# Recurrent attention with streamed weights: 14 buffers hold two weight pieces by turns, head halves swap order, softmax by rows, and a separate stage for the batched tokens' output projection

## The chip, the cores and the metric

One core of a Trainium2 chip runs one program. The metric is the device time of one execution in microseconds. The engines are TensorE (PE), VectorE (DVE), ScalarE (ACT), GpSimd (POOL) and SyncE (SP); DMAs are issued from the queues of SP, ACT and POOL.

## The reference, cut to what matters

```
x: [2048, 1024]; Wq, Wk, Wv: [1024, 32 heads, 128]; Wo: [32, 128, 1024]
mem = mem0                                   # 8 rows
for s in range(64):                          # 32 tokens per segment
    h = concat(mem, x[32*s : 32*s + 32])     # 40 rows
    q, k, v = h @ Wq, h @ Wk, h @ Wv         # per head
    scores = where(idx_q < 8 or idx_q >= idx_k, q k^T * 128**-0.5, -1e9)
    o = softmax(scores) @ v, then @ Wo       # 40 x 1024
    mem = o[:8];  outs.append(o[8:])
a = concat(outs)
b = (gelu(x @ w_gate) * (x @ w_up)) @ w_down # 3584 hidden columns
g = sigmoid(sum(x * gate_w))
out = g * a + (1 - g) * b
```

All inputs and the output are bf16. The 64 segments depend on each other through `mem`, so they run one after the other. The four weight matrices of the attention are 8 MB each, 32 MB together, and more than the on-chip buffers hold.

## The kernel before, in words

**Three stages.** A prologue loads and transposes x, computes the gate, and computes q, k and v of the "rest" tokens: of each segment's 32 tokens the last 8 (`NB`) are projected in one batch for all segments, 512 rows, and written to scratch tensors in HBM (`qk_scr`, `v_scr`). Then comes the loop over 64 steps (one segment each), whose projections carry 32 rows: 24 tokens of the segment and the 8 memory rows. Last comes the feed-forward stage (matmuls at L941 and L978), which also mixes in the attention result.

**Pieces.** Each weight matrix is cut into 16 pieces of 512 KB ([128, 2048] bf16): half `u` of the heads (16 heads) times 8 slices of the contraction (for Wo: 8 pairs of heads per half). A step walks all 64 pieces in the order of `pos` (L301): k half 0, q half 0, k half 1, q half 1, v half 0, v half 1, then Wo half 0 and half 1. A q, k or v piece is four matmuls of 32 output rows by 512 columns (L793), one for each quarter of the PE's columns, which run side by side. A Wo piece is eight matmuls of 256 columns (L819), two rounds of four.

**Residents and ring.** 44 pieces stay in SBUF for the whole loop (`res`). The other 20 (`streamed`, L308) are loaded again in each step into a ring of 5 buffers (`ring`). `load_str` (L342) issues the next ring load on SP's queue when the piece that held the buffer has been used; SP's instructions run in the order in which they were written, so a load waits for its buffer and all later loads wait behind it.

**Softmax.** The batched tokens' columns of k and q are put beside the step's own (`put_rest`, POOL, from `qkr`). For each half `u`, `scores` (L686) computes masked scores with queries on partitions only for the row maximum (DVE, L700). `scores_T` computes them again with keys on partitions. `shift` and `denom` subtract the maximum and sum over keys by matmuls with a block matrix of ones, with two exponentials and a logarithm on ACT (L741, L753, L759). `attend` (L762) multiplies by v, and four copies (ACT and DVE by turns) bring the result to `oT`.

**Order of the work.** Helpers are hung on piece numbers (`on(n, f)`, L841 on): they are written into the program ahead of piece n. Each engine runs its instructions in program order and waits on semaphores.

**Wo.** Each step multiplies all 32 rows by Wo into bank A0. The 8 batched tokens' rows are collected over four steps (`keep_o` into `oTR`), and in every fourth step `proj` does a second set of matmuls for them with the same pieces, into bank A1 (`lag`), which POOL stores (`a_scr<-a_rb`).

**End of a step.** The Wo result is copied to `a_bf` (half by ACT, half by DVE), transposed on the PE (L890) and copied by DVE into the memory columns of the next step's `hT` (L893); the next step's first matmul waits for that copy.

**Prologue details that the change touches.** The q and k results of the rest tokens are gathered in `stq` and stored to `qk_scr` by a DMA on ACT's queue, 2 MB in runs of 256 B. Some v pieces are loaded into `tmpv`, which lies over `stq`, by SP (L571). The v results go to `v_scr` by SP's DMAs from `stv` (L558).

Of the kernel before, what the change touches and what calls it, by code (L numbers as in the profile page):

```python
# [195 lines left out]
def bass_gated_mix__memory_aug_recurrent_mem_tr__geglu_ffn__prompt_kernel(  # L196
# [19 lines left out]
    SEG = 32  # L216
# [8 lines left out]
    NRING = 5  # L225
# [6 lines left out]
    with ExitStack() as es:  # L232
# [12 lines left out]
        v_scr = nc.dram_tensor("v_scr", [NSEG // 2, 4, 32, 512], BF16)  # L245
# [19 lines left out]
        bones = al("bones", [128, 128])  # L265
        delta = al("delta", [128, 32])
        mS = al("mS", [128, 80])
        mT = al("mT", [128, LQ])
        mR = al("mR", [128, 4, 16])
        gal = al("gal", [128, NT], FP32)  # L270
        hT = [al(f"hT{i}", [128, KC, 32]) for i in range(2)]
        a_bf = al("a_bf", [128, 256])
        nm = [al(f"nm{u}", [128, 4, 2], FP32) for u in range(2)]
        qkr = al("qkr", [128, 4, 128])
        oTR = [al(f"oTR{u}", [128, 4, 4, 32]) for u in range(2)]
        a_rb = al("a_rb", [128, 256], at=oTR[0].off)
        low = cur[0] = (cur[0] + 63) // 64 * 64
        vB = al("vB", [128, 4, 128])

        xb = [al(f"xb{i}", [128, 640]).off for i in range(4)]  # L280
        kT = [al(f"kT{u}", [128, 4, 4, LQ], at=xb[(0, 2)[u]]) for u in range(2)]
        qT = [al(f"qT{u}", [128, 4, 4, LQ], at=xb[1]) for u in range(2)]
        DDs = [al(f"DD{u}", [128, 4, LQ], at=xb[(0, 2)[u]]) for u in range(2)]
        EE = [al(f"EE{u}", [128, 4, 56], at=xb[(0, 2)[u]]) for u in range(2)]
        LN = [al(f"LN{u}", [128, 4, LQ], FP32, at=xb[(0, 2)[u]] + 448) for u in range(2)]
        oT = [al(f"oT{u}", [128, 4, 4, LQ], at=xb[(1, 0)[u]]) for u in range(2)]
        tok = al("tok", [128, 512], at=xb[3])
        vA = [al(f"vA{u}", [128, 4, 128], at=xb[3]) for u in range(2)]
# [12 lines left out]
        pos = [(m, u, kc) for m, u in QUADS for kc in range(KC)]  # L301
        pos += [("o", u, g, jj) for u in range(2) for g in range(4) for jj in range(2)]
        assert len(pos) == 64
        at_, tot = [], 0
        for p in range(64):
            tot += 1 + extra.get(p, 0)
            at_.append(tot)
        streamed = [(at_[p] * NSTR) // tot > ((at_[p - 1] if p else 0) * NSTR) // tot for p in range(64)]  # L308
        assert sum(streamed) == NSTR
        res = {p: al(f"res{p}", [128, 2048]) for p in range(64) if not streamed[p]}  # L310
        str_pos = [p for p in range(64) if streamed[p]]
        str_qkv = [p for p in str_pos if p < 48]
        seq = [p for p in str_qkv if p < 32] + str_pos * NSEG
# [16 lines left out]
        def dst(t, p):  # L330
            return t[:, :].rearrange("p (h f) -> p h f", h=2) if pos[p][0] == "o" else t[:, :]
# [692 lines left out]
```

## Time and profile before

| what | value |
|---|---|
| median of 3 runs | 2887.17 us (2876.43 to 2901.04) |
| span of the profiled execution, its own time | 2881.1 us |
| PE busy | 2355.2 us (82%) |
| DVE, ACT, POOL busy | 757.5 us (26%), 627.0 us (22%), 337.8 us (12%) |
| DMA bytes | 838.19 MB, mean 291 GB/s |
| chain that ended last, by engine | DMA 47%, PE 43%, issue 4%, DVE 2% |
| chain, longest lines | ring<-Wq 17%, ring<-Wv 13%, L941 11%, L793 11%, L819 8%, ring<-Wk 7%, ring<-Wo 6% |

The profiled execution has no time of its own beside its span; the median of the timed runs is 6.1 us above the span. "Busy" is the union of an engine's instructions, and pipelined matmuls overlap, so a busy PE is not a PE at its peak rate. In a chain row, "DMA x" means that the work at that point waited for that transfer to land. Releasers are inferred.

### The profile page before, as it was taken

The page shows a single profiled execution, that of the slowest core. Times are in us where ns is not written, and L with a number is a line of the kernel's source. Part 1 is how long each engine was busy: PE and PEld are TensorE (multiplying, and loading weights), DVE is VectorE, ACT ScalarE, POOL GpSimd, SP SyncE. Part 2 cuts the span into 40 slices and gives each one's busy share as a digit, 9 for nine tenths or more (in the row PEclk, how much of TensorE's full clock was granted, in tenths as well). Part 3 has the DMA queues.
Part 4 walks back from the last instruction along what each step waited for, and adds up shares of the span by engine and source line. Part 5 has one row for each costly group of instructions (what it writes and reads, how often), then busy time and mean ns, then how long its engine had stood idle before and what let it go on. Part 6 is the DMA issues. An engine that isn't in the chain of part 4 may idle for free.

```text
span 2881.1 us, 88022 instructions
## 1 busy us (share of the span) xinstructions
PE 2355.2 (82%) x40448; PEld 1097.0 (38%) x40486; DVE 757.5 (26%) x1829; ACT 627.0 (22%) x1461; POOL 337.8 (12%) x775
## 2 busy tenths in 40 slices
PE   7687788787787877787787877787777899999998
PEld 3333333343333333333343333333333444444443
DVE  1411222112222212222222221222212353526262
ACT  1211222222222222222222221222222231303130
POOL 2400111111111111111111111111111000000000
PEclk9888998999999999999999999999999999999999
DMA  9546999999999999999999999999999926070705
GB/s 336 168 155 237 368 356 341 321 333 348 341 362 345 377 345 342 363 349 361 335 343 351 335 351 333 361 345 342 347 331 357 367 78 225 1 245 4 245 4 190
DMA packets 338595, 838.19 MB, mean 291 GB/s; under 512 B 65193, under 2 KB 79529, under 8 KB 338225
## 3 DMA queue, kind: packets, MB, share of 16 engines
q1 hardware_dynamic: 284512, 789.16, 76.3%
q0 software_dynamic: 13824, 22.16, 2.4%
q10 hardware_dynamic: 39888, 21.24, 2.4%
q8 instruction: 317, 5.19, 0.7%
q14 instruction: 54, 0.43, 0.0%
HBM read 806.11 MB, written 26.21 MB: 289 GB/s over the span
## 4 chain that ended last, share of the span: by engine, by line
DMA 47%; PE 43%; issue 4%; DVE 2%; ACT 1%; POOL 1%; ACTq 1%; SPq 0%; POOLq 0%
DMA ring<-in_A_Wq_dram 17%; DMA ring<-in_A_Wv_dram 13%; PE pb L941 11%; PE pb L793 11%; PE pb L819 8%; DMA ring<-in_A_Wk_dram 7%; DMA ring<-in_A_Wo_dram 6%; PE pb L978 6%; PE pb L517 2%; DMA wd<-in_B_w_down_dram 1%; PE pb L545 1%; PE pb L674 1%; POOL gp L475 1%; DMA qk_scr<-stq 1%; ACTq L472 1%
## 5 line engine op out<-in xcount | busy, mean ns | idle before, releaser
L793 PE MATMUL pb<-res,hT 128*32 128x512 bf16 x8448 | 671.2, 404 | 2.0 <-issue 2.0
L793 PE MATMUL pb<-ring,hT 128*32 128x512 bf16 x3840 | 403.1, 409 | 286.1 <-DMA ring<-in_A_Wk_dram 103.7
L793 PEld LDWEIGHTS pb<-ring,hT 128*32 128x32 bf16 x3840 | 102.0, 95 | 487.6 <-DMA ring<-in_A_Wk_dram 165.5
L793 PEld LDWEIGHTS pb<-res,hT 128*32 128x32 bf16 x8448 | 215.6, 100 | 165.6 <-issue 43.2
L819 PE MATMUL pb<-res,oT 128*32 128x256 bf16 x5632 | 247.7, 281 | 37.7 <-issue 37.4
L657 ACT ACTIVATE tok<-pb 128x512 bf16<-128x512 f32 (+1 forms) x256 | 139.2, 544 | 583.0 <-PE pb L793 577.5
L941 PE MATMUL pb<-xT,wg 128*128 128x512 bf16 x896 | 211.8, 379 | 9.5 <-DVE GT L957 8.4
L941 PE MATMUL pb<-xT,wu 128*128 128x512 bf16 x896 | 211.7, 379 | 0.0
L978 PE MATMUL pb<-wd,GT 128*128 128x512 bf16 x876 | 194.2, 379 | 7.4 <-DMA wd<-in_B_w_down_dram 6.1
L819 PE MATMUL pb<-ring,oT 128*32 128x256 bf16 x2560 | 140.9, 283 | 54.0 <-DMA ring<-in_A_Wo_dram 24.6
L819 PEld LDWEIGHTS pb<-res,oT 128*32 128x32 bf16 x5632 | 150.8, 99 | 60.0 <-issue 49.0
L949 ACT ACTIVATE s<-pb 128x512 f32<-128x512 f32 x112 | 66.8, 596 | 316.2 <-PE pb L941 296.7
L831 POOL COPY oTR<-oT 128x128 bf16<-128x128 bf16 x128 | 37.6, 294 | 828.3 <-DVE oT L660 828.3
L700 DVE TENSOR_REDUCE nm<-pb 128x8 f32<-128x320 f32 x128 | 63.0, 492 | 270.4 <-PE pb L696 270.4
L941 PEld LDWEIGHTS pb<-xT,wg 128*128 128x128 bf16 x896 | 86.9, 98 | 117.5 <-DVE GT L957 12.8
L978 PEld LDWEIGHTS pb<-wd,GT 128*128 128x128 bf16 x896 | 86.7, 98 | 115.0 <-DMA wd<-in_B_w_down_dram 12.0
L941 PEld LDWEIGHTS pb<-xT,wu 128*128 128x128 bf16 x896 | 87.7, 98 | 105.7
L657 ACT ACTIVATE oT<-pb 128x160 bf16<-128x160 f32 x256 | 63.8, 301 | 273.6 <-PE pb L774 273.6
L660 DVE CAST oT<-pb 128x160 bf16<-128x160 f32 x256 | 71.2, 320 | 197.9 <-PE pb L774 197.9
L826 POOL COPY qT<-qkr 128x128 bf16<-128x128 bf16 x128 | 45.0, 351 | 587.6 <-PE pb L720 582.5
L950 DVE SCALAR_TENSOR_TENSOR tp<-s,pb 128x512 f32<-128x512 f32 x112 | 77.0, 687 | 137.2 <-ACT s L949 137.1
L819 PEld LDWEIGHTS pb<-ring,oT 128*32 128x32 bf16 x2560 | 61.4, 97 | 119.9 <-issue 56.3
(106 smaller groups left out, 2493.0 us busy)
## 6 DMA issues: line engine op xcount, KB each, us to landing
ring<-in_A_Wk_dram SPq DMA_DIRECT2D x325, 512.0 KB, 6.2
ring<-in_A_Wq_dram SPq DMA_DIRECT2D x325, 512.0 KB, 7.2
ring<-in_A_Wv_dram SPq DMA_DIRECT2D x320, 512.0 KB, 6.7
ring<-in_A_Wo_dram SPq DMA_DIRECT2D x320, 512.0 KB, 6.7
wd<-in_B_w_down_dram SPq DMA_DIRECT2D x56, 1024.0 KB, 6.0
qk_scr<-stq ACTq DMA_DIRECT2D x4, 2048.0 KB, 11.6
qkr<-qk_scr POOLq DMA_DIRECT2D x64, 128.0 KB, 6.1
res<-in_A_Wk_dram SPq DMA_DIRECT2D x11, 512.0 KB, 12.2
```

Source lines behind the costliest of these rows:

```text
L517: ins = e.matmul(PB[b][:, 0:NRT], lhsT=w8[kc][:, c:c + 128], rhs=xrT[:, kc, :], start=(kc == 0), stop=(kc == KC - 1))
L657: op("act", lambda e: e.activation(o, i, ACTF.Copy), rd=rd, wr=wr)
L660: op("dve", lambda e: e.tensor_copy(o, i), rd=rd, wr=wr)
L700: op("dve", lambda e: e.tensor_reduce(nm[u][:, :, :].rearrange("p a b -> p (a b)"), PB[SS][:, 0:320].rearrange("p (a c) -> p a c", c=LQ), ...
L793: ins = e.matmul(PB[bk][32 * g:32 * g + 32, :], lhsT=h[:, kc, :], rhs=w[:, g * 512:(g + 1) * 512], start=(kc == 0), stop=(kc == KC - 1))
L819: ins = e.matmul(PB[bk][32 * g:32 * g + 32, 0:256], lhsT=o[u][:, gp_, 2 * jj + hh, 0:32], rhs=w[:, c:c + 256], start=(p == 48 and hh == 0) ...
L826: op("pool", lambda e: e.tensor_copy(t[:, :, :, 32:40].rearrange("p j g c -> p (j g) c"), qkr[:, m, :].rearrange("p (x c) -> p x c", c=8)) ...
L831: op("pool", lambda e: e.tensor_copy(oTR[u][:, :, :, 8 * i:8 * i + 8].rearrange("p g j c -> p (g j) c"), oT[u][:, :, :, 32:40].rearrange(" ...
L941: ins = e.matmul(PB[bk][:, 0:FB], lhsT=w[:, kc, cc:cc + 128], rhs=xT[:, :, :, kc, :].rearrange("p t i c -> p (t i) c"), start=(kc == 0), s ...
L949: op("act", lambda e, hg=hg: e.activation(s1[:, :], hg, ACTF.Square, scale=SQ), rd=[BK(bg)], wr=[s1.r()])
L950: op("dve", lambda e, hg=hg, t=t: e.scalar_tensor_tensor(out=t[:, :], in0=s1[:, :], scalar=1.0, in1=hg, op0=ALU.add, op1=ALU.mult), rd=[BK ...
L978: ins = e.matmul(PB[bank[2 * k + hf]][:, :], lhsT=GT[:, j, tb * 128:(tb + 1) * 128], rhs=w[:, jj, hf * 512:(hf + 1) * 512], start=(j == 0) ...
```

## The change

The 5 ring buffers are gone. There are 50 buffers (`slots`); 36 hold one piece for good, and 14 (`PAIRS`: 3 of k, 3 of q, 4 of v, 4 of Wo) hold the pieces of both head halves with the same contraction slice by turns. A step takes half `s % 2` first and the other half second, so the half that a shared buffer holds at the end of a step is the one that the next step begins with. `spent` issues the reload of a shared buffer behind the use of its piece.

The order of a step becomes k, q, v of the first half, k and q of the second, Wo of the first, v of the second, Wo of the second (`ORDER`). Only one set of `kT`, `qT`, `oT`, `tok` remains, and many small tiles lie over each other (`pA`, `pB` over `kT`; `E8`, `tA`, `tB` over `qT`; `a_bf` over `oT`; `vA` over `tok`).

The softmax works on the scores with queries on partitions: maximum, subtraction in PSUM, one exponential, sum, reciprocal, two multiplications, and two 32x32-block transposes, all but the exponential on DVE. `scores_T`, `shift` and `denom` with their masks are gone.

The batched tokens' rows of `oT` are collected in `oRc` and stored to `o_scr` in each step; a new stage between the loop and the feed-forward stage loads them (`oR`), reloads four Wo pieces (`xo`) and does 256 matmuls of 512 columns. In the prologue the halves are taken in the other order, v_scr is stored in runs of 256 B, and reloads follow `spent`.

```diff
-        ring = [al(f"ring{i}", [128, 2048]) for i in range(NRING)]
...
+        ORDER = (("k", 0), ("q", 0), ("v", 0), ("k", 1), ("q", 1), ("o", 0), ("v", 1), ("o", 1))
+        walk = [(m, r, i) for m, r in ORDER for i in range(8)]
+        def at_step(p, s):
+            m, r, i = (pos if s < 0 else walk)[p]
+            return (m, r ^ (s % 2), i)
+        PAIRS = {"k": (1, 3, 5), "q": (0, 2, 5), "v": (0, 2, 4, 6), "o": (0, 2, 4, 6)}
...
+        def fetch(n):
+            k, t = uses[n][done[n]], slots[n]
+            if paired(k):
+                lane = f"sl{n}"
...
+            op("sp", lambda e: e.dma_start(dst(t, k), src(k)), wr=[t.r()], lane=lane)
+        def spent(k):
+            n = home[k]
+            done[n] += 1
+            if done[n] < len(uses[n]) and uses[n][done[n]] != k:
+                fetch(n)
...
+            op("pool", lambda e: e.memset(pB[:, :].bitcast(FP32), 0.0), wr=[pB.r()])
+            op("dve", lambda e: e.tensor_reduce(nm, sS, AX.X, ALU.max, negate=True), rd=[BK(SS)], wr=[st8.r(0, 8)])
+            op("dve", lambda e: e.tensor_tensor(out=sS, in0=sS, in1=b8(nm, LQ), op=ALU.add), rd=[BK(SS), st8.r(0, 8)], wr=[BK(SS)])
+            op("act", lambda e: e.activation(E8[:, :, :].rearrange("p a c -> p (a c)"), PB[SS][:, 0:320], ACTF.Exp, scale=scale),
+               rd=[BK(SS)], wr=[E8.r()])
+            op("dve", lambda e: e.tensor_reduce(sm, E8[:, :, :], AX.X, ALU.add), rd=[E8.r()], wr=[st8.r(8, 16)])
+            op("dve", lambda e: e.reciprocal(sm, sm), rd=[st8.r(8, 16)], wr=[st8.r(8, 16)])
+            op("dve", lambda e: e.tensor_tensor(out=pA[:, :, :], in0=E8[:, :, 0:32], in1=b8(sm, 32), op=ALU.mult),
+               rd=[E8.r(), st8.r(8, 16)], wr=[pA.r()])
+            fin = op("dve", lambda e: e.tensor_tensor(
...
+            op("dve", lambda e: e.transpose(tA[:, :, :].rearrange("p a c -> p (a c)"), pA[:, :, :].rearrange("p a c -> p (a c)")),
+               rd=[pA.r()], wr=[tA.r()])
+            op("dve", lambda e: e.transpose(tB[:, :, :].rearrange("p a c -> p (a c)"), pB[:, 0:256]),
+               rd=[pB.r()], wr=[tB.r()], after=[fin])
...
         def attend(u):
-            bo = (T1, SS, (ST0, ST1)[u], XX)
+            bo = (B0, B1, B2, SS)
...
+                for g in range(4):
+                    r = slice(32 * g, 32 * g + 32)
+                    ins = e.matmul(PB[bo[g]][:, 0:4 * LQ].rearrange("p (j c) -> p j c", j=4)[:, :, 24:40], lhsT=vB[r, u, :],
...
+            op("pool", lambda e: e.tensor_copy(oRc[:, :, 16 * u:16 * u + 16].rearrange("p c x -> p x c"),
+                                               oT[:, :, :, 32:40].rearrange("p g j c -> p (g j) c")),
+               rd=[oT.r()], wr=[oRc.r()])
...
             def start_step():
-                put_rest(kT[0], 1)
-                put_rest(qT[0], 0)
-                put_rest(kT[1], 3)
+                put_rest(kT, 1)
+                put_rest(qT, 0)
                 for f in pend:
                     f()
                 pend.clear()
...
+                load_qk(s, 1)
+            def rest_1():
+                put_rest(kT, 1)
+                put_rest(qT, 0)
+                if not last:
+                    load_qk(s + 1, 0)
+            on("k", 0, 2, start_step)
+            on("k", 0, 5, lambda: load_h(s + 1) if not last else None)
+            on("q", 0, 0, lambda: evac(bko["k", 0], tok, "act"))
+            on("q", 0, 4, lambda: trans(kT, "dve"))
+            on("v", 0, 0, lambda: evac(bko["q", 0], tok, "act"))
+            on("v", 0, 3, lambda: trans(qT, "dve"))
+            on("v", 0, 7, lambda: scores())
+            on("k", 1, 0, lambda: evac(bko["v", 0], vA, "act"))
+            on("q", 1, 4, lambda: attend(ua))
+            on("q", 1, 5, lambda: rest_1())
+            on("q", 1, 5, lambda: evac(bko["k", 1], tok, "act"))
+            on("q", 1, 7, lambda: trans(kT, "dve"))
+            on("o", 0, 0, lambda: evac(bko["q", 1], tok, "act"))
+            on("o", 0, 3, lambda: trans(qT, "dve"))
+            on("o", 0, 7, lambda: scores())
+            on("o", 1, 0, lambda: evac(bko["v", 1], vA, "act"))
+            on("o", 1, 0, lambda: attend(ub))
+            on("o", 1, 0, lambda: load_v(s + 1) if not last else None)
...
-            act_copy(a_bf[:, 0:128], PB[A0][:, 0:128], [BK(A0)], [a_bf.r(0, 128)])
-            dve_copy(a_bf[:, 128:256], PB[A0][:, 128:256], [BK(A0)], [a_bf.r(128, 256)])
+            act_copy(a_bf[:, :], PB[XO][:, 0:256], [BK(XO)], [a_bf.r()])
...
+                op("pool", lambda e: e.dma_start(o_scr[s], oRc[:, :, :].rearrange("p c x -> p (c x)")), rd=[oRc.r()],
+                   wr=[("D", "o", s)], lane="sto")
...
+        load_oR(NBK - 1)
+        for b in range(NBK):
+            rb = rbs[b % 2]
+            for hf in range(2):
...
+                    for n, (u, i, hh) in enumerate((u, i, hh) for u in range(2) for i in range(8) for hh in range(2)):
+                        w = xo.get(("o", u, i)) or slots[home["o", u, i]]
+                        x = 16 * u + 2 * i + hh
+                        ins = e.matmul(PB[bk][0:RB, :], lhsT=oR[b][:, :, x],
+                                       rhs=w[:, hh * 1024 + hf * 512:hh * 1024 + hf * 512 + 512], start=(n == 0), stop=(n == 31))
...
+        load_w(2)
         load_w(3)
         load_w(4)
```

In the last step `early` holds `load_xo`, three `load_oR`, `load_xT(0)`, `load_w(0)` and `load_w(1)`; `oR` and `xo` lie over the buffers of v.

## Rows read from the trace of the kernel before

**Rows 1.** The page, 40 equal slices: busy share of the DMA engines, in tenths.

```profile
DMA  9546999999999999999999999999999926070705
```

**Rows 2.** The page, DMA issues: count, KB each, median us from issue to landing.

```profile
ring<-in_A_Wk_dram SPq DMA_DIRECT2D x325, 512.0 KB, 6.2
ring<-in_A_Wq_dram SPq DMA_DIRECT2D x325, 512.0 KB, 7.2
ring<-in_A_Wv_dram SPq DMA_DIRECT2D x320, 512.0 KB, 6.7
ring<-in_A_Wo_dram SPq DMA_DIRECT2D x320, 512.0 KB, 6.7
...
qk_scr<-stq ACTq DMA_DIRECT2D x4, 2048.0 KB, 11.6
...
a_scr<-a_bf POOLq DMA_DIRECT2D x64, 64.0 KB, 5.8
```

**Rows 3.** Tile hT: the copy that opens each next step, first and last start.

```profile
L893 DVE COPY hT<-pb x63: 191/192/193, 291.4 to 2238.4; 128x64 bf16<-128x64 bf16 x63
```

**Rows 4.** Stretches: us, PE, PEld, DVE, ACT, POOL busy, PEclk, DMA share, GB/s.

```profile
1050.00:1350.00 300.00, 234.56 (x5622) 109.55 (x5614) 65.55 (x207) 68.76 (x180) 41.95 (x99) 0.99 0.98 358
20.00:40.00 20.00, 19.95 (x91) 8.76 (x92) 3.77 (x6) 3.15 (x6) 6.54 (x24) 1.00 1.04 400
1578.90:1610.30 31.40, 25.47 (x532) 11.41 (x532) 6.64 (x21) 6.38 (x17) 3.63 (x9) 0.82 0.94 332
```

**Rows 5.** Timeline 1400 to 1435 us: start, us, engine, line, operation.

```profile
1404.42 0.38 PE L696 MATMUL pb<-kT,qT 128*32 128x40 bf16 x32
...
1413.75 1.06 PE L819 MATMUL pb<-res,oT 128*32 128x256 bf16 x32
...
1415.26 0.28 ACT L657 ACTIVATE a_bf<-pb 128x128 bf16<-128x128 f32 x1 [2.27 <-PE pb L819]
...
1416.48 0.40 PE L793 MATMUL pb<-ring,hT 128*32 128x512 bf16 x4 [0.28 <-DVE hT L893]
...
1418.82 1.04 PE L793 MATMUL pb<-res,hT 128*32 128x512 bf16 x16
...
1419.79 0.40 PE L674 MATMUL pb<-ident,tok 128*128 128x128 bf16 x4
...
1425.06 1.50 PE L793 MATMUL pb<-res,hT 128*32 128x512 bf16 x12
```

**Rows 6.** DMA issues, 186 to 200 us, the queue empty at first: us to landing.

```profile
tmpv<-in_A_Wv_dram SPq DMA_DIRECT2D x1, 512.0 KB, 4.3
```

**Rows 7.** Groups by shape, 1350 to 1650 us: busy, mean ns | idle before.

```profile
L700 DVE TENSOR_REDUCE nm<-pb 128x8 f32<-128x320 f32 x18 | 8.9, 492 | 35.5 <-PE pb L696 35.5
L756 DVE SCALAR_TENSOR_TENSOR pb<-pb,LN 128x160 f32<-128x160 f32 x18 | 6.0, 333 | 6.2 <-ACT LN L753 6.1
L657 ACT ACTIVATE tok<-pb 128x512 bf16<-128x512 f32 x30 | 17.9, 597 | 84.1 <-PE pb L793 84.1
```

**Rows 8.** PE's waits in the prologue, 0 to 262 us.

```profile
PE pb L517 <- DMA ring<-in_A_Wq_dram: 26.2, 1, 26.2
PE pb L545 <- ACT stv L552: 10.5, 1, 10.5
```

**Rows 9.** Timeline of SP's queue, 110 to 262 us.

```profile
134.32 0.33 SPq L571 DMA_DIRECT2D tmpv<-in_A_Wv_dram  x1
...
136.82 1.49 SPq L349 DMA_DIRECT2D ring<-in_A_Wq_dram  x2
...
189.84 0.33 SPq L571 DMA_DIRECT2D tmpv<-in_A_Wv_dram  x1
```

**Rows 10.** Timeline of PE, 244 to 270 us: the loop's first matmuls.

```profile
245.48 0.40 PE L793 MATMUL pb<-ring,hT 128*32 128x512 bf16 x4
```

**Rows 11.** The chain that ended last: feed-forward begins, and 49 matmuls of it.

```profile
2274.29 25.86 PE pb L941 x119
...
2822.43 10.74 PE pb L978 x49
```

More of the change, by code (lines that the diff above doesn't have):

```diff
@@ L284, in bass_gated_mix__memory_aug_recurrent_mem_tr__geglu_ffn__prompt_kernel @@
[L284 to L288, printed above, removed]
+        low = cur[0] = (cur[0] + 63) // 64 * 64
+        qkr = al("qkr", [128, 2, 128])
+        oRc = al("oRc", [128, NB, 32])
@@ new lines, in bass_gated_mix__memory_aug_recurrent_mem_tr__geglu_ffn__prompt_kernel @@
+        PAIRS = {"k": (1, 3, 5), "q": (0, 2, 5), "v": (0, 2, 4, 6), "o": (0, 2, 4, 6)}
+        hosts = []
+        for m in "kqvo":
+            for i in range(8):
+                if i in PAIRS[m]:
+                    hosts.append([(m, 0, i), (m, 1, i)])
+                else:
+                    hosts += [[(m, 0, i)], [(m, 1, i)]]
+        assert len(hosts) <= NSLOT, (len(hosts), NSLOT)
+        slots = [al(f"sl{n}", [128, 2048]) for n in range(len(hosts))]
+        home = {p: n for n, h in enumerate(hosts) for p in h}
@@ L315, in bass_gated_mix__memory_aug_recurrent_mem_tr__geglu_ffn__prompt_kernel @@
+        paired = lambda p: len(hosts[home[p]]) > 1
+        uses = [[] for _ in hosts]
+        for s_ in [-1] + list(range(NSEG)):
+            for p in range(48 if s_ < 0 else 64):
+                k = at_step(p, s_)
+                if s_ < 0 and k[0] == "v" and paired(k) and k[1] == 1:
+                    continue
+                uses[home[k]].append(k)
         P = _Prog(nc, new_sem, "a")
@@ L500, in bass_gated_mix__memory_aug_recurrent_mem_tr__geglu_ffn__prompt_kernel @@
         for n, (mat, u) in enumerate(QUADS):
-            w8 = [tmpv.get(8 * n + kc) or piece(8 * n + kc) for kc in range(KC)]
+            u = 1 - u
+            k8 = [(mat, u, kc) for kc in range(KC)]
+            w8 = [tmpv.get(k) or slots[home[k]] for k in k8]
             if mat != "v":
@@ L860, in bass_gated_mix__memory_aug_recurrent_mem_tr__geglu_ffn__prompt_kernel @@
-            on(26, lambda: scores(0))
-            on(28, lambda: scores_T(0, s % 2))
-            on(29, lambda: trans(tok, T0, kT[1], "act"))
-            on(32, lambda: evac(A1, tok, "both"))
-            on(32, lambda: shift(0))
-            on(35, lambda: trans(tok, T1, qT[1], "both"))
-            on(36, lambda: denom(0))
-            on(40, lambda: scores(1))
-            on(40, lambda: cp["act"](vA[0][:, :, :].rearrange("p j c -> p (j c)"), PB[A0][:, :], [BK(A0)], [vA[0].r()]))
-            on(41, lambda: scores_T(1, s % 2))
@@ L870, in bass_gated_mix__memory_aug_recurrent_mem_tr__geglu_ffn__prompt_kernel @@
-            on(44, lambda: attend(0))
-            on(44, lambda: keep_o(0, s % 4))
-            on(46, lambda: shift(1))
-            on(48, lambda: cp["dve"](vA[1][:, :, :].rearrange("p j c -> p (j c)"), PB[A1][:, :], [BK(A1)], [vA[1].r()]))
-            on(49, lambda: denom(1))
-            on(55, lambda: attend(1))
-            on(55, lambda: keep_o(1, s % 4))
-            on(56, lambda: load_v(s + 1) if s % 2 and not last else None)
+                load_qk(s, 1)
[4 more added lines that the diff above has]
+                    load_qk(s + 1, 0)
```

384 lines of the change are left out of this document (146 added, 238 removed).

## The prediction

> **What bounds the kernel now.** I read the page first. Its chain of waits is 47% DMA, nearly all of it ring loads, though PE is busy 82% of the span; so the busy share misleads, and the 40 slices say why: through the loop the DMA engines stand at 9 tenths in every slice [rows 1]. The list of DMA issues shows what they carry: 1,290 ring loads of 512 KB [rows 2], 20 in each of 64 steps and 10 in the prologue. The copy that opens a step runs from 291.4 to 2238.4 us [rows 3], 62 steps of 31.40 us. Twenty loads at the loop's 358 GB/s (DMA share 0.98) [rows 4] are 20 x 1.46 = 29.3 us, and about 1 us of small transfers makes 30.3: the loop is bound by reload bytes. PE's own work is far less: four pieces take 1.04 us with their drain and one takes 0.40 [rows 5], so a piece costs 0.213 us and 64 pieces 13.6 us.
>
> **Part 1, the reloads.** By the code a shared buffer changes its piece once in a step, between the first and the second half, so 14 reloads replace 20. They are no longer spread evenly: ten (k, q, v) are released in the first 24 pieces and queue up, and the four of Wo queue behind them. SP's next reload always belongs to a later release, so a blocked SP delays nothing. PE never outruns the last Wo reload by my count below, so a step is one round through it:
> - after that reload lands, two Wo pieces and their drain: 2 x 0.213 + 0.19 = 0.62 us;
> - the step's end to the next first matmul: now 1.22 us (1415.26 to 1416.48) [rows 5]. ACT copies twice the columns (0.28 grows to about 0.38) and the 0.30 of DVE behind it goes: 1.0 us;
> - k pieces 0 and 1, whose second releases the first reload: 0.62 us;
> - issue 0.1 us, and landing from an idle queue 4.3 us [rows 6]; the nearest other row is a ring load's 6.2 us behind others [rows 2], the upper end;
> - 13 more reloads. In the loop the rate is 358 GB/s, with up to five loads in flight; in the prologue, with more queued, 400 [rows 4]. That bounds one between 1.31 and 1.46 us. Ten will be queued here, but small transfers run beside them: I take the middle, 1.38, so 17.9 us;
> - six small transfers of 64 KB (hT, k and q of two halves, v, two stores), 1.0 us; they could fall into the pause of the reloads and cost nothing.
>
> Sum 25.5 us; with the low ends 23.7, with the high ends 28.5 (small transfers 1.0 and 1.2 us more for a slower clock at the round's PE parts). 63 steps: 1606 us.
> The Trainium skill ("DMA: Bandwidth & Descriptors", section "Where 436 GB/s comes from") says that loads from HBM are bound near 358 GB/s per core. The trace has 400 in one stretch [rows 4]; by the page's figure the step would be 26.6 us and the total some 70 us higher.
>
> **Part 2, the softmax.** PE loses `scores_T`, `shift`, `denom` and the second Wo set; all of it lay beside loads and gives nothing by itself. What is added is serial: from the end of `scores` DVE reduces (0.49 us [rows 7]), adds over 320 columns in PSUM (between 0.33, its 160-column neighbour, and 0.49; I take 0.49), ACT's exponential of 320 columns (under 0.60; 0.44), reduce 0.49, reciprocal 0.15, multiplications 0.33 and 0.2, two transposes that no row shows (0.2 to 0.5 each; 0.35), hand-overs 0.3: C = 3.6 us, from 2.6 to 7.2 if everything new is twice as dear. Cover of the first half: 12 pieces, 2.6 us; of the second: 9 pieces, 1.95 us. PE's serial path without any DMA wait is then 13.6 + transposes 4 x 0.2 + scores 2 x 0.5 [rows 5] + attends 0.8 + end 1.0 + stalls behind the copies of tok (0.60 each [rows 7]) and oT 1.9 + (C - 2.6) + (C - 1.95) = 14.6 + 2C = 21.8 us. That is below 25.5, so reloads cover it; without them it would be the step. Queued behind new waits: on ACT the copy of v behind the exponential (q's first piece needs its bank); on POOL `put_rest` behind the `oRc` copy (the k copy of DVE waits for it, under 1 us). A store of `a_bf` now holds `oT`, but lands in 5.8 us [rows 2], and `attend` comes some 11 us into the step. POOL also gets one memset per half, one more store and more loads; it idles most of the step.
>
> **Part 3, the prologue.** PE now waits 26.2 us for a ring load of Wq [rows 8], which SP issues at 136.82 only behind `tmpv` (134.32), which waits for a store of `stq` [rows 9]. The new order issues those q pieces a quad earlier: gone. The 10.5 us wait behind the first store of `stv` [rows 8] is SP stuck at the same line; v pieces will still queue ahead of that store, so I take half. Gain 31 us, between 10 and 37. v_scr in runs of 256 B costs nothing: `stq`, in such runs, takes 11.6 us for 2 MB [rows 2], so 0.7 us per 128 KB store, beside 55 us of matmuls (8 blocks of 32 at 0.219); without that cover, 23 us. The loop then begins at 245.5 [rows 10] - 31 = 214.5. In step 0 the twelve Wo pieces that had no room before load ahead of its 14 reloads: 26 x 1.38 + 4.4 + 1.0 + 2.2 = 43.5 us; it ends at 258, against 291.4.
>
> **Part 4, the new Wo stage.** In the last step the four `xo` pieces and the first `oR` can start only when v's buffers are free, behind the Wo reloads: 4 x 1.38 + 4 (1 MB in 512 B runs, 2.6 to 5.8 us by 400 GB/s and by the `stq` row) = 9.5 us, less 1.0 that the loop's tail covers: 8.5. Then 256 matmuls at 10.74 / 49 = 0.219 us [rows 11]: 56.1 us, on the path. The last `oR` load waits for the last store, with w2 to w4 and wd behind it on SP; the stage covers those, and w3 is wanted some 48 us into the feed-forward stage. Now the same multiplications hide under loads, and only 1.7 us lie between loop and feed-forward. Together 65 us.
>
> **Sum.** 258 + 63 x 25.5 + 65 + feed-forward as before (2881.1 - 2274.3 = 606.8) [rows 11] = 2536 us against the profiled 2881.1. The timed median is 6.1 us above that span, so 2542.
>
> **Rivals.**
> 1. *The serial softmax sets the step.* From C = 5.4 us PE's path passes 25.5. At C = 7.2 the step is 29.0 and the time 2542 + 63 x 3.5 = 2760. For it: both halves share one set of buffers, so nothing else fills PE. Against: each new operation has a near neighbour below 0.5 us [rows 7].
> 2. *Reloads cheaper than thought.* If the landing overlaps and the rate is above 400 GB/s, PE's 21.8 us is the step: 2542 - 63 x 3.7 = 2310. Against: the last Wo reload is tied to a release late in the step.
> 3. *Slower: PE's clock stays low.* The waits now bunch, in q of the second half and in the last Wo pieces. At 1.2 GHz twelve matmuls of three pieces take 1.50 us [rows 5], about 0.43 a piece. If that held, the path would be 27.3 of pieces + 7 of the rest, 34.5 us a step, and the time 2542 + 63 x 9 = 3110. It decides against the change where a step passes (2881 - 607 - 65 - 258) / 63 = 31.0 us, a mean granted clock near 0.6. Against: before, with waits for loads too, stretches have 0.99, and one of the lowest steps 0.82 [rows 4]. The Trainium skill ("TensorE: Matmul & The Clock Gate", section "What's actually happening") calls the half rate the default that activity lifts; the trace agrees that the clock falls after waits, and shows it coming back.
>
> That the reloads don't fall to 14 I exclude: the count follows from the code.
>
> **Chances.** Forecast 0.82 (its own range 2430 to 2720: the step's ends, -1.8 and +3.0 us times 63, with the prologue's and the new stage's partly offsetting), rival 1 beyond that 0.09, rival 2 0.05, rival 3 0.04. Runs of this kernel spread by about 1%, so 1% is what can be told from no change. Faster by over 1% is all but rival 3 and a little of rival 1: 0.94; the same 0.02, slower 0.04.
>
> **What would show it.** Right: 14 shared-buffer loads a step, hT copies 25.5 us apart, PE waiting in the last Wo pieces for shared buffers of Wo, a pause of the DMA engines around each step's start, and 56 us of 512-column Wo matmuls. Wrong: PE waiting for the transposed probabilities ahead of `attend` while its next reload has landed (rival 1); the last Wo pieces without a wait (rival 2); granted clock under 0.7 in the loop (rival 3); PE still idle for 20 us near 130 us (part 3).

## The result, and the profile after

The kernel before took 2881.8 us in the median of four runs, the changed one 2735.4 (2718.4 to 2737.6): a ratio of 0.948, 95% interval 0.943 to 0.953. The forecast was 2542, with a range that ended at 2720. The change made the kernel faster, as forecast; what failed is the length of a step.

The profiled execution has a span of 2735.8 us. Tile `hT`: the copy that opens each next step, for all steps and for the last 41.

```profile
L839 DVE COPY hT<-pb x63: 190/192/193, 249.1 to 2033.7; 128x64 bf16<-128x64 bf16 x63
...
L839 DVE COPY hT<-pb x41: 191/192/192, 879.5 to 2033.7; 128x64 bf16<-128x64 bf16 x41
```

Sixty-two steps take 1784.6 us, 28.78 each, against 31.40 [rows 3] and a forecast of 25.5. That is 203 us. All other parts together are within 5 us of the sum: step 0 ends at 249.1 (258 forecast), from the last copy to the feed-forward stage's first matmul (2127.34) pass 93.6 us (25.5 + 65 forecast), and the feed-forward stage takes 608.5 (606.8).

The page: clock and DMA share in 40 slices, the longest lines of the chain, and the reloads (count, KB, us to landing).

```profile
PEclk9998988899888899988888888889799999999999
DMA  8678787787877778878778787778788343250705
...
DMA sl<-in_A_Wq_dram 23%; PE pb L758 14%; DMA sl<-in_A_Wo_dram 13%; PE pb L905 12%; PE pb L770 7%; PE pb L942 6%; PE pb L673 2%; PE pb L864 2%; PE pb L529 2%; PE pb L501 2%; DMA wd<-in_B_w_down_dram 2%; ACT tok L656 1%; ACT a_bf L656 1%; SPq L347 1%; PE pb L836 1%
...
sl<-in_A_Wv_dram SPq DMA_DIRECT2D x268, 512.0 KB, 11.4
sl<-in_A_Wo_dram SPq DMA_DIRECT2D x268, 512.0 KB, 6.4
sl<-in_A_Wk_dram SPq DMA_DIRECT2D x208, 512.0 KB, 7.1
sl<-in_A_Wq_dram SPq DMA_DIRECT2D x208, 512.0 KB, 9.5
```

Where every slice of the loop stood at 9 [rows 1], the DMA engines now stand at 7 or 8: they pause. Of the reloads, Wq and Wo are left among the chain's longest lines; Wv, 13% before, is not. One step's reload issues on SP's queue (a step from 1252.84 to 1282.18) show 14 of them:

```profile
1253.50 2.45 SPq L347 DMA_DIRECT2D sl<-in_A_Wk_dram  x3
1255.99 2.19 SPq L347 DMA_DIRECT2D sl<-in_A_Wq_dram  x3
1258.23 1.98 SPq L347 DMA_DIRECT2D sl<-in_A_Wv_dram  x4
...
1269.19 2.31 SPq L347 DMA_DIRECT2D sl<-in_A_Wo_dram  x4
```

Between the last v issue and the first Wo issue lie 9 us. The chain of waits through the same step (start, us, what):

```profile
1255.94 1.25 PE pb L758 x21
1257.19 8.34 DMA sl<-in_A_Wq_dram
...
1265.58 1.04 PE pb L758 x6
...
1269.63 0.40 PE pb L673 x4
1270.02 1.02 PE pb L770 x32
1271.04 0.02 issue
1271.06 8.78 DMA sl<-in_A_Wo_dram
1279.84 0.14 issue
1279.97 1.07 PE pb L770 x14
```

This step waits for two reloads one after the other, with PE's work between them: a q reload lands, PE goes through the rest of q and the first half's Wo, only that releases the Wo buffers, and the last of their reloads takes 8.8 us more. It is not so in every step. In the one that ended at 1223.90 the chain has the q reload too, but then the softmax in place of the Wo reload, and Wo's second half behind it:

```profile
1199.22 9.01 DMA sl<-in_A_Wq_dram
...
1218.61 0.34 DVE tB L717
...
1219.82 3.22 PE pb L770 x64
```

PE's waits from 1200 to 1500 us (total, times, longest; 10.4 steps):

```profile
PE pb L727 <- DVE tB L717: 18.0, 10, 1.8
PE pb L758 <- DMA sl<-in_A_Wk_dram: 16.4, 19, 2.2
PE pb L758 <- DMA sl<-in_A_Wq_dram: 13.4, 20, 1.5
PE pb L770 <- DMA sl<-in_A_Wo_dram: 7.7, 12, 1.0
```

Once in each step PE waits 1.8 us for the transposed probabilities (rival 1's sign), and in 38 of 54 steps it then waits for Wo too (the forecast's sign). Mean granted clock, DMA share and GB/s (last three columns) over the loop, in the step's first 5 us and in its last:

```profile
300.00:1900.00 1600.00, 1224.91 (x24663) 574.16 (x24663) 490.60 (x1387) 312.12 (x722) 348.18 (x779) 0.88 0.78 270
...
1252.00:1257.00 5.00, 4.45 (x78) 2.12 (x82) 0.62 (x2) 0.84 (x3) 2.36 (x4) 1.00 0.44 102
...
1277.00:1282.00 5.00, 3.10 (x50) 1.53 (x50) 0.07 (x1) 0.38 (x1) 1.47 (x5) 0.63 0.10 38
```

### The profile page after: what moved, and what is told of

Its sections match the earlier page's. It is cut to its first block, busy times and chain, and to the rows that moved or that the text cites. A ratio compares the mean times of both kernels' runs of the same rounds, so it can differ in the third digit from the quotient of the medians.

```text
span 2735.8 us, 71514 instructions
## 1 busy us (share of the span) xinstructions
PE 2236.5 (82%) x32250; PEld 1046.5 (38%) x32294; DVE 900.9 (33%) x2089; ACT 540.3 (20%) x1129; POOL 437.9 (16%) x931
## 4 chain that ended last, share of the span: by engine, by line
PE 49%; DMA 39%; DVE 5%; ACT 3%; issue 2%; SPq 1%; ACTq 1%; POOL 1%; POOLq 0%
DMA sl<-in_A_Wq_dram 23%; PE pb L758 14%; DMA sl<-in_A_Wo_dram 13%; PE pb L905 12%; PE pb L770 7%; PE pb L942 6%; PE pb L673 2%; PE pb L864 2%; PE pb L529 2%; PE pb L501 2%; DMA wd<-in_B_w_down_dram 2%; ACT tok L656 1%; ACT a_bf L656 1%; SPq L347 1%; PE pb L836 1%
## 5 line engine op out<-in xcount | busy, mean ns | idle before, releaser
L758 PE MATMUL pb<-sl,hT 128*32 128x512 bf16 x12288 | 905.2, 422 | 211.1 <-DMA sl<-in_A_Wk_dram 96.5
L758 PEld LDWEIGHTS pb<-sl,hT 128*32 128x32 bf16 x12288 | 309.7, 101 | 603.2 <-issue 159.9
L770 PE MATMUL pb<-sl,oT 128*32 128x256 bf16 x8192 | 346.6, 311 | 78.4 <-DMA sl<-in_A_Wo_dram 49.3
L770 PEld LDWEIGHTS pb<-sl,oT 128*32 128x32 bf16 x8192 | 223.4, 107 | 155.0 <-issue 91.3
L656 ACT ACTIVATE tok<-pb 128x512 bf16<-128x512 f32 x256 | 153.4, 599 | 397.7 <-PE pb L758 392.7
L741 POOL COPY oRc<-oT 128x128 bf16<-128x128 bf16 x128 | 96.0, 750 | 764.3 <-DVE oT L659 764.3
L704 ACT ACTIVATE E<-pb 128x320 bf16<-128x320 f32 x128 | 55.9, 437 | 417.9 <-DVE pb L703 417.9
L905 PEld LDWEIGHTS pb<-xT,wg 128*128 128x128 bf16 x896 | 86.8, 98 | 116.5 <-DVE GT L921 12.8
L501 PE MATMUL pb<-xrT,sl 128*128 128x512 bf16 x499 | 117.1, 390 | 5.2 <-DMA sl<-in_A_Wq_dram 2.5
L673 PE MATMUL pb<-ident,tok 128*128 128x128 bf16 x1024 | 111.6, 238 | 8.9 <-ACT tok L656 2.6
L673 PEld LDWEIGHTS pb<-ident,tok 128*128 128x128 bf16 x1024 | 63.6, 104 | 136.1 <-ACT tok L656 121.3
```

The costliest lines, as they stand in the source:

```text
L501: ins = e.matmul(PB[b][:, 0:NRT], lhsT=w8[kc][:, c:c + 128], rhs=xrT[:, kc, :], start=(kc == 0), stop=(kc == KC - 1))
L656: op("act", lambda e: e.activation(o, i, ACTF.Copy), rd=rd, wr=wr)
L673: ins = e.transpose(PBV[TT][:, j * 128:(j + 1) * 128], tok[:, j * 128:(j + 1) * 128], ident[:, :])
L704: op("act", lambda e: e.activation(E8[:, :, :].rearrange("p a c -> p (a c)"), PB[SS][:, 0:320], ACTF.Exp, scale=scale), rd=[BK(SS)], wr=[E ...
L741: op("pool", lambda e: e.tensor_copy(oRc[:, :, 16 * u:16 * u + 16].rearrange("p c x -> p x c"), oT[:, :, :, 32:40].rearrange("p g j c -> p ...
L758: ins = e.matmul(PB[bk][32 * g:32 * g + 32, :], lhsT=h[:, i, :], rhs=w[:, g * 512:(g + 1) * 512], start=(i == 0), stop=(i == KC - 1))
```

## The experiments

"Step" is the time between two `hT` copies, the mean from the first to the last of the loop unless another stretch is named; ratios are to the kernel before, with their 95% interval. The runs of the changed kernel (2718.4 to 2737.6 us) spread by 0.3 us a step, so a difference of 0.3 us tells nothing. The theory at first was the forecast's: a step is one round through the reload queue, with a term too small. Its rivals: PE's serial path with the softmax sets the step, or the clock does.

**e1_small_late.** Four small transfers on POOL's queue (two stores, `load_qk`, `load_h`) wait for the first half's seventh q piece.

```diff
+            def small():
+                late = [mark["q", 0, 6]]
...
-                    f()
+                    f(after=late)
...
-                load_qk(s, 1)
+                load_qk(s, 1, after=late)
+                if not last:
+                    load_h(s + 1, after=late)
-            on("k", 0, 5, lambda: load_h(s + 1) if not last else None)
+            on("q", 0, 7, small)
```

> The five small transfers that POOL issues at the start of a step (stores of a_bf and oRc, loads of qkr and hT) are held back until the seventh q piece of the first half is done. In the changed kernel the mean step of 28.77 us splits into 0.86 (start to first reload issue), 6.15 (its landing), 12.73 (nine more landings), 2.02, 4.91 (to the last Wo reload) and 2.11 (to the next start). Theory A, small transfers stand in front of the first reloads: its landing falls from 6.15 to 4.1-4.9 us, the step by 1.2 to 1.7 us, the time by 75 to 105 us. Rival C, the DMA engines start slowly after a pause whatever is queued: the landing stays at 6.15, and the small transfers now slow the reloads in the middle, so the time stays or rises by up to 60 us.

2778.7 us, 0.963 (0.958 to 0.968), step 29.26. The first reload landed 4.05 us after its issue in place of 6.15 (means of 54 steps), as theory A had it, but the nine behind it took 15.29 in place of 12.73. Moved among the loads, the transfers cost more than they gave back.

**e2_fill** and **e7_fill_kq.** Matmuls without use ahead of the pieces where PE waits: 18 a step ahead of k, q and Wo, then 12 ahead of k and q alone.

```diff
+        FILL = (("k", 1, 2), ("k", 3, 2), ("k", 5, 2), ("q", 0, 3), ("q", 2, 3), ("o", 2, 2), ("o", 4, 2), ("o", 6, 2))
...
+            for m_, i_, n_ in FILL:
+                on(m_, 1, i_, lambda n_=n_: fill(n_, ua))
```

> Eighteen filler matmuls of 512 columns per step, on a bank that is free, ahead of the pieces at which PE waits for a reload (k 1, 3, 5 and q 0, 2 of the second half, Wo 2, 4, 6); nothing of the computation changes. Theory A with the clock as one cause: the granted clock in the loop rises from 0.87 to over 0.95, the end of the round falls from 2.11 to about 1.65 us and the first issue from 0.86 to 0.75, the step by 0.6 to 1.0 us, the time by 40 to 65 us. If the clock costs nothing (waits alone): no change. Rival B, PE's own serial path is the step: fillers are added work, 18 x 0.216 = 3.9 us, of which at least 2 us a step show, 125 us slower.

> Fillers as in e2 but ahead of the k and q pieces alone (12 a step), where PE waits longest. In e2 the granted clock of the loop rose from 0.88 to 0.97 and the Wo release came 0.7 us earlier, but the end of the round grew from 2.11 to 2.83 us. If the fillers ahead of the last Wo pieces did that: end back to 2.1 or less, step 0.3 to 0.8 us shorter than 28.77, 20 to 50 us less. If the low clock costs nothing on this path: no change.

e2: 2750.2 us, 0.954 (0.949 to 0.959), step 29.06. e7: 2709.4, 0.940 (0.936 to 0.943), step 28.14. The loop's clock rose from 0.88 to 0.97 in both. With fillers in front of k and q alone a step is 0.6 us shorter, the fillers' own time paid; those in front of Wo gave it back: from the last Wo landing to the step's end passed 2.83 us in e2, 2.11 in the changed kernel. e2's step is no shorter than the changed kernel's, where theory A had 0.6 to 1.0, and not 2 us longer, as rival B had.

**e3_attend_early.** The first half's `attend` two pieces earlier, and what hangs behind it two or three.

```diff
-            on("q", 1, 4, lambda: attend(ua))
...
-            on("q", 1, 7, lambda: trans(kT, "dve"))
+            on("q", 1, 2, lambda: attend(ua))
...
+            on("q", 1, 5, lambda: trans(kT, "dve"))
```

> The first half's attend, with the copies behind it, moves from the fifth to the third q piece of the second half, where PE waits for a q reload, and the transpose of k from the eighth to the sixth. Theory A (the Wo reloads are released too late, 17.05 us into the step, when the v reloads are nearly through): release at about 15.8, the gap between the last v landing and the first Wo landing falls from 2.02 to about 1.45, the step by 0.4 to 0.6 us, the time by 25 to 40 us. If Wo's reloads only queue behind v's, or rival B: no change within 10 us.

2699.5 us, 0.937 (0.933 to 0.942), step 28.11. Of the reloads' releases this moves that of Wo (issued 16.50 us into the step, from 17.05), and the step is 0.67 us shorter.

**e4_softmax_1us.** The row maximum is computed three times, 1 us more in each half.

```diff
+            for _ in range(3):
+                red = op("dve", lambda e: e.tensor_reduce(nm, sS, AX.X, ALU.max, negate=True), rd=[BK(SS)], wr=[st8.r(0, 8)],
+                         after=[red] if red else ())
```

> The row maximum is computed three times in a row, which lengthens the serial softmax of each half by 2 x 0.5 = 1.0 us; the output is the same. Theory A: in the first half attend waits for q reloads, not for the softmax, in the second the delay is absorbed by the 1.6 us that PE waits for Wo reloads: step +0 to +0.3 us, time 0 to 20 us slower. Rival B, the softmax path sets the step: +1.0 to +2.0 us a step, 63 to 125 us slower.

2772.8 us, 0.960 (0.954 to 0.966), step 29.41: of 2 us added, 0.6 reach the step, between the two theories' ranges. The softmax is on the path for part of the time.

**e5_small_idle** and **e6_idle_attend.** Three small transfers go into the pause at the step's end, behind the second half's third Wo piece, and the `put_rest` copies of the next step with them; e6 adds e3's edit.

```diff
-                load_qk(s, 1)
+            def idle():
+                put_rest(kT, 1)
+                put_rest(qT, 0)
+                store_o(s, [mark["o", 1, 2]])
+                if s + 2 < NSEG:
+                    load_h(s + 2)
+                load_qk(s + 1, 1)
+            on("o", 1, 3, idle)
```

> The store of oRc and the loads of hT (for the step after next) and qkr move from the start of the step to the pause of the DMA engines at its end, behind the third last-half Wo piece; only the store of a_bf stays at the start. e1 showed that the first reload lands after 4.05 us instead of 6.15 when the small transfers are away, and that four of them take some 2.1 to 2.6 us of the DMA engines wherever they stand among reloads. Theory A': their price, not their place, is what the sum had too low, and only the pause can hide it: landing 4.3-5.0 us, the ten loads stay near 12.8, the Wo reloads suffer at most 0.5 us, step 0.8 to 1.5 us shorter, time 50 to 95 us less than 2735. Rival: the softmax path of the second half is as long as the reload chain, so the step gains under 0.4 us, 25 us.

> Both e3 (first attend two pieces earlier, step 28.77 to 28.05 us) and e5. If the two gains lie on one chain one after the other they add: step 26.6 to 27.2 us, 2600 to 2645 us. If both only uncover the same next limit (softmax of the second half): about as the better of the two alone, 2670 to 2700.

e5: 2684.4 us, 0.931 (0.929 to 0.934), step 27.96. e6: 2660.3, 0.923 (0.919 to 0.927), step 27.54. The edits alone (e5, e3) gave 0.82 and 0.67, both together 1.24: less than the sum, more than the better one.

**e8_no_swap.** Every step takes half 0 first, so each shared buffer changes its piece twice: 28 reloads.

```diff
-            return (m, r ^ (s % 2), i)
+            return (m, r ^ (s < 0), i)
```

> The halves are taken in the same order in every step, so each of the 14 shared buffers is reloaded twice a step, 28 reloads; all else as in the changed kernel. By the reload price of 1.41 us (12.73 / 9) and about 2.5 us for small transfers, if the reloads set the step: 28 x 1.41 + 2.5 = 42 us a step, 38 to 44, total 3320 to 3700 us: the swap is what makes the change pay. If PE's path set the step: about 29 us, 2740.

3350.8 us, 1.163 (1.161 to 1.166), step 38.50: the swap is what makes the change pay. Here the queue does set the step, and shows its rate over 1200 us (DMA share and GB/s last):

```profile
600.00:1800.00 1200.00, 772.07 (x13854) 332.36 (x13858) 274.85 (x777) 175.20 (x405) 196.26 (x438) 0.77 1.03 393
```

At 393 GB/s a reload is 1.33 us, and 14 of them 18.7; the changed kernel's 28.8 cannot be a queue that is always full.

**e9_idle_attend_fill.** e6 with e7's fillers.

> The three edits that each gained, together: the first half's attend three pieces earlier, three small transfers moved to the step's end, and 12 filler matmuls a step ahead of waits for k and q. If each takes its own term off one serial round, the 27.54 us step of the two-edit kernel falls by the fillers' 0.70 to 26.8, and the time to about 2615. If two chains of nearly the same length take turns, as the two-edit kernel (-1.23 of -1.55) hinted, by half of that: 27.2 and 2640. Granted clock 0.96 or more in the loop either way.

2671.7 us, 0.927 (0.923 to 0.930), step 27.66, clock 0.94 over 300 to 1900 us: no gain over e6, where 0.3 to 0.7 were expected. Three edits that each gave 0.6 to 0.8 give 1.1 together, which terms of one sum would not do; that hints at another form and does not show it. The next runs leave parts out.

**e10_no_small, e11_no_reload, e12_no_v_reload.** From step 20 on no load of `hT`, `qkr`, `vB` and from step 16 on no store of `o_scr`; from step 2 on no reload at all; and none of v.

```diff
+            if s >= 20:
+                return
...
-            if done[n] < len(uses[n]) and uses[n][done[n]] != k:
+            if done[n] < len(uses[n]) and uses[n][done[n]] != k and not (now[0] >= 2 and paired(k)):
```

> From step 20 on, five of the six small transfers of a step are left out (hT, the two loads of qkr, the load of vB, the store of o_scr; old data is used again, and the new stage reads the first 16 steps' stores), so that their whole price is seen with nothing put in another place. If they cost what the prediction said (1.0 for six), the step falls from 28.78 by 0.8 to 28.0. If they are the mis-sized term (about 2 us in front of the first landing, and no pause to hide in), by 1.5 to 2.5, to 26.3 to 27.3, with the first landing 4.0 to 4.5 us behind its issue. If the first landing stays at 6 us, the slow start has another cause.

> From step 2 on no shared buffer is reloaded (the second half of the heads is multiplied with what the buffers hold), so PE, DVE and ACT run their step with no wait for a reload. The prediction's sum for this path is 21.8 us; with DVE's and ACT's rows of the changed kernel it stays 21 to 23. A step in this range means that the reloads' chain is some 6 us longer and alone sets the end. A step of 25 or more means that PE and the softmax by themselves nearly fill the 28.8, and that the prediction's PE path was mis-sized too.

> From step 2 on the four v buffers are not reloaded (ten reloads a step in place of 14). If the step is one serial round through the reloads, it falls by four landings of 1.27 us each, to 23.7. If PE's path to the second attend, and so the release of the Wo buffers, is nearly as long as the reloads' queue, it falls by 1 to 3 us only, to 26 to 28: the Wo reloads are then issued behind their own release, and not behind the queue.

Tile `hT` in the steps without, in this order:

```profile
L845 DVE COPY hT<-pb x41: 190/192/192, 870.8 to 1983.5; 128x64 bf16<-128x64 bf16 x41
```

```profile
L842 DVE COPY hT<-pb x60: 190/192/192, 319.8 to 1729.3; 128x64 bf16<-128x64 bf16 x60
```

```profile
L842 DVE COPY hT<-pb x61: 190/191/193, 305.2 to 2013.4; 128x64 bf16<-128x64 bf16 x61
```

e10: 1112.7 / 40 = 27.82 us against 28.86 in the same steps of the changed kernel: five small transfers cost 1.0, the forecast's figure, and were not the mis-sized term. The first landing came 4.7 us after its issue, still above 4.3. e11: 1409.5 / 59 = 23.89, PE's path by itself, not 21.8; it lies above the range of 21 to 23 and below the 25 of the other reading. e12: 1708.2 / 60 = 28.47: four reloads of fourteen left out, and only 0.3 us gone, which is no more than the spread of runs (5.5 by the sum; the expectation had at least 1). The queue of 14 is not what a step waits for. (Times 2692.0, 2428.0, 2709.8 us; ratios 0.933 (0.928 to 0.938), 0.842 (0.838 to 0.846), 0.940 (0.934 to 0.945).) PE's longest waits in e11 from 1200 to 1500 us (12.6 steps):

```profile
PE pb L729 <- DVE tB L719: 29.5, 25, 1.8
PE pb L839 <- ACT a_bf L658: 6.3, 13, 0.5
```

**e15_no_kq_reload, e16_no_wo_reload.** The same with the reloads of k and q, and of Wo, left out.

```diff
+            if done[n] < len(uses[n]) and uses[n][done[n]] != k and not (now[0] >= 2 and paired(k) and k[0] in "kq"):
```

> From step 2 on the six shared buffers of k and q are not reloaded (v and Wo are). Theory A: the wait of 3.9 us ahead of the first Wo piece goes, the rest stays: step 25 to 25.5. Theory B (queue): eight reloads are left, 28.8 - 6 x 1.27 = 21.2, so PE's path of 23.9 would be the step.

> From step 2 on the four shared buffers of Wo are not reloaded. Theory A: what they add behind PE's own second half, about 1 us: step 27.6 to 28.2. Theory B (queue): the last landing is that of v at 19.7 us behind the step's start, with PE's end of the step behind it; PE's path of 23.9 would be the step.

```profile
L842 DVE COPY hT<-pb x60: 190/192/192, 324.6 to 1747.0; 128x64 bf16<-128x64 bf16 x60
```

```profile
L842 DVE COPY hT<-pb x61: 190/192/193, 301.9 to 1958.0; 128x64 bf16<-128x64 bf16 x61
```

e15: 1422.4 / 59 = 24.11 us; e16: 1656.1 / 60 = 27.60 (2447.5 and 2650.9 us; 0.848 (0.842 to 0.855) and 0.919 (0.911 to 0.927)). e16 is as theory A (waits in series on PE's path) had it, and against theory B, the queue (23.9). e15 alone does not tell them apart: 24.11 is below A's 25 to 25.5 and nearest to the queue's 23.9; it is e12 and e16 that rule the queue out. Without k and q a step is 0.2 us above e11's, so the reloads of k and q cost 4.7 us, those of Wo 1.2, those of v no more than the spread. They add to more than the 4.9 between 28.8 and 23.9. Part of the delay therefore goes with either group: Wo's reloads cost 1.2 us where k and q are reloaded too, but Wo's and v's together only 0.2 where they are not. In the mean of 54 steps the first Wo matmul starts 16.7 us after the copy that opens the step, 16.6 in e16, but 12.8 in e11 and 12.7 in e15.

Not all of this is waiting. PE's busy time, clock, DMA share and GB/s over the same stretch of the changed kernel, e11 and e15:

```profile
500.00:1700.00 1200.00, 916.15 (x18535) 0.88 0.78 272
```

```profile
500.00:1700.00 1200.00, 993.15 (x22337) 0.94 0.07 19
```

```profile
500.00:1700.00 1200.00, 951.32 (x22107) 0.99 0.57 193
```

That is 22.0, 19.8 and 19.1 us of busy PE in a step for the same work. Of the 4.9 us between the changed kernel and e11, 2.7 are idle PE and 2.2 are busier PE; of the 4.7 between it and e15, 1.8 and 2.9. So the late reloads cost PE time twice, by the wait and by slower work around it. How much of the busier part is the lower clock, and how much matmuls that run alone between waits, was not separated.

**e13_shared_first_last** and **e14_order_idle.** If k and q are the costly reloads, PE has to meet them later, and they have to be issued earlier. In a step's first half the shared buffers' slices come first (earlier reloads), in the second last (PE has its private pieces done when it begins to wait). e14 adds e5's edit.

```diff
+        def turn(m, r):
+            a, b = list(PAIRS[m]), [i for i in range(8) if i not in PAIRS[m]]
+            return b + a if r else a + b
-        walk = [(m, r, i) for m, r in ORDER for i in range(8)]
+        walk = [(m, r, i) for m, r in ORDER for i in turn(m, r)]
```

> Only the order of the eight slices inside each block of pieces is changed: the shared buffers' slices come first in a step's first half, so that their reloads are issued earlier, and last in its second half, so that PE has all private pieces done when it begins to wait. Theory A (a step is PE's serial path of 23.9 us, plus about 3.9 of waiting for the six k and q reloads ahead of the first Wo piece, plus about 1 for the Wo reloads behind it): the wait for q comes with one piece left in place of three, and the four Wo reloads are issued within 0.8 us in place of 2.1. Step 26.5 to 27.3, time 2600 to 2650. Theory B (one queue of 14 reloads sets the step): the queue starts 0.2 us earlier and ends with one piece behind it in place of two, so 28.3, and 2705.

> The same order, with three small transfers moved to the pause of the reloads at the step's end. Theory A: the first reload lands 1.5 us earlier, and 0.5 to 0.8 of that reaches the wait for q: step 25.9 to 26.7, time 2560 to 2610. Theory B: 27.5, and 2655.

e13: 2607.7 us, 0.903 (0.898 to 0.909), step (1894.4 - 245.9) / 62 = 26.59. e14: 2563.6 us (2552.2 to 2574.3), 0.887 (0.881 to 0.894), step 26.20, the fastest here. All 14 reloads remain; both steps lie in the ranges that waits in series gave (theory A) and below what one queue gave. The loop's clock rose with them, to 0.93 and 0.94. In e14 the wait for q is down to a third a step in this stretch, and most of the rest stands at DVE's softmax and at Wo (1200 to 1500 us, 11.5 steps):

```profile
PE pb L732 <- DVE tB L722: 18.2, 19, 1.8
PE pb L777 <- DMA sl<-in_A_Wo_dram: 12.9, 17, 1.1
...
PE pb L765 <- DMA sl<-in_A_Wq_dram: 4.1, 7, 1.1
PE pb L765 <- DMA sl<-in_A_Wk_dram: 4.0, 4, 2.0
```

## Why the prediction was wrong

**The step failed, in its form.** The text had "a step is one round through" the last Wo reload, counted the other 13 behind the first at 1.38, and set PE's path beside them ("below 25.5, so reloads cover it"). The runs show a series: PE's own path of 23.9 us (e11), and on top of it 4.9 us that the reloads add, 4.7 of them gone when k and q alone are not reloaded (e15). By the order of a step PE uses k and q of the second half before it may use the first half's Wo, and only that use releases the Wo buffers. So a late q is also a late Wo release, while v's reloads, which the sum charged 4 x 1.38, cost no more than the spread of runs (e12). With 23.9 for 21.8 and 4.9 in series, the step is 28.8. The forecast's larger-of-two had no such case.

**The terms, in the sum's own order** (means over 54 steps of the changed kernel): first reload issued 0.86 us after the end of the copy that opens the step (0.62); it lands 6.15 us later, where the sum had 0.1 + 4.3 and 1.0 for the small transfers; nine more landings 12.73 (9 x 1.38 = 12.4); from the last v to the first Wo 2.02 (1.38), since Wo is issued only 17.05 us into the step; three more Wo 4.91 (4.1); to the end of the next copy 2.11 (1.62). The excess is spread over all terms, which is why the queue looked like the cause until v's reloads were left out.

**PE's path: form right, 2.1 us low.** The softmax chain was C = 3.6 us; it takes 3.5, and the transposes for which no row stood are within their 0.2 to 0.5 (first and last rows on DVE, the first behind the scores):

```profile
1259.66 0.49 DVE L702 TENSOR_REDUCE st<-pb 128x8 f32<-128x320 f32 x1 [1.18 <-PE pb L697]
...
1262.42 0.44 DVE L715 STREAM_TRANSPOSE tA<-pA 128x256 bf16<-128x256 bf16 x1
1262.78 0.40 DVE L717 STREAM_TRANSPOSE tB<-pB 128x256 bf16<-128x256 bf16 x1
```

The forecast let it stall PE for 1.0 + 1.65 us; in e11 PE waits for `tB` 29.5 / 12.6 = 2.3. What was low lies elsewhere on PE's path: the 13.6 us for 64 pieces came from rows at the full clock, and e11 falls below it at the end of most steps. The last eight Wo pieces there, in one step and in another (us, PE busy, clock, DMA share, GB/s):

```profile
1201.06:1202.99 1.93, 1.93 (x64) 1.00 0.03 8
1247.76:1250.96 3.20, 3.20 (x64) 0.57 0.07 26
```

In 13 of 54 steps they take 1.93 us at a clock of 1.00, and most of these steps take 22.7 us; in the other 41 they take 2.9 to 3.6 at 0.52 to 0.63, and the steps 24.1 in the mean. So somewhat over half of the 2.1 us is the lower of the two clock levels, right behind the wait for `tB`; the other 0.9 was not divided.

**Rival 1** was given 0.09, at C = 5.4 or more. C stayed at 3.5, yet its sign is in the profile in every step: the wait for `tB`. It was half true: softmax and reloads take turns at the end of a step.

**Rival 2** is out: taking all reloads away leaves 23.9. **Rival 3** did not show its sign, a clock under 0.7: it is 0.88 in the loop. But its mechanism has a part that the sum set at nothing, since every term of its PE path was at the full clock: over half of what PE's own path has too much, and some of the 4.9 us behind it. Lifting the clock to 0.97 by fillers gave 0.6 us a step. The Trainium skill ("TensorE: Matmul & The Clock Gate", section "What's actually happening") calls the half rate the default that activity lifts; e2 and e7 agree, where added matmuls raised the clock from 0.88 to 0.97.

**Prologue and new stage: cause right, the prologue's gain too low.** SP's stuck order is gone (134.13 us, then reloads at once), and the longest wait for Wq that is left there is 2.5 us of the 26.2:

```profile
134.13 0.33 SPq L559 DMA_DIRECT2D tmpv<-in_A_Wv_dram  x1
134.50 0.43 SPq L347 DMA_DIRECT2D sl<-in_A_Wv_dram  x1
```

The loop begins at 204.4 us (214.5 forecast). The gain is 41 us, above the forecast's 10 to 37: the half of the wait behind the `stv` store [rows 8] that was thought to stay, 5 us, went too, and the other 5 were not traced. The new stage waits 8.5 us, the forecast's figure, and then runs 56.7 us to 2127.34:

```profile
2061.11 1.04 PE L770 MATMUL pb<-sl,oT 128*32 128x256 bf16 x16 [0.46 <-DMA sl<-in_A_Wo_dram]
2070.67 4.86 PE L864 MATMUL pb<-sl,oR 128*128 128x512 bf16 x15 [8.52 <-DMA oR<-o_scr]
```

Here the terms agree too: the first `oR` landed 9.1 us behind the last Wo reload that PE waited for (9.5 in the sum), and 1.0 of them was covered. The 6.1 us between span and median of before did not come back: 2735.8 and 2735.4.

**The range** reached to a step of 28.5, and that is a slip in the sum. The high ends, 0.62 + 1.0 + 0.62 + 0.1 + 6.2 + 13 x 1.46 + 1.0, make 28.5 without the 1.2 us for a slower clock that the text adds to them; with it they make 29.7, and the range would have ended near 2800. It would then have held the 2735.4, but by its width alone: it took in the ends of the landings, and not that a PE path and a queue could add.

## What to carry to other kernels

Before taking the larger of a compute path and a queue of loads, follow each release: where a late load holds back the very work that releases the next buffers, the two add. What a group of loads costs is told by leaving that group out, not by its bytes or by where the landings are late: here four of fourteen cost nothing that could be told from the spread, and six cost 4.7 us. Read the clock beside each such run, for a wait can also slow the work behind it. What helped was order, not fewer bytes: shared buffers first where they are released, last where they are awaited.

## What the runs showed of the hardware

- Reloads start slowly after a pause. In the 5 us from the first issue of the step shown (1253.50) the DMA engines move 209 GB/s at a share of 0.73, and in the mean of 54 steps the first 512 KB land 6.2 us after their issue, where at e8's rate they would take 1.33. With few or no small transfers beside them they land after 4.1 (e1) and 4.7 us (e10), about the 4.3 of [rows 6], so the small transfers are most of what came on top of that. Why 4 us are left was not tried.
- The end of a burst is slow too. From 1277 to 1282 us the share is 0.10, between one and two of the 16 engines. In every place of the step the last engine of a reload lands 1.3 to 2.1 us behind the eighth, in the mean. Why was not tried.
- One core's transfers reached 393 GB/s over 1200 us (e8), of which the 28 reloads of a 38.5 us step are 381. The Trainium skill ("DMA: Bandwidth & Descriptors", section "Where 436 GB/s comes from") says that loads from HBM are bound near 358 GB/s per core; the measurement here is higher, and decides.
- POOL's copy of `oT` into `oRc` takes 0.75 us for 128 columns, where ACT's copies of 160 columns take 0.30. POOL has 1% of the chain that ended last.
